# A fused attention and MLP kernel: another split of the last token tile, another wait ahead of the weight loads, and another ranking of all planned steps

## The chip, the cores and the metric

One core of a Trainium2 chip runs the kernel. The metric is device time in microseconds (us), the median of eight runs. The profile is one more execution, taken by the hardware profiler. Engines are named as the profile names them: PE is TensorE with its matmuls, PEld its weight loads, DVE is VectorE, ACT is ScalarE, POOL is GpSimd, SP is SyncE (which here only issues DMAs). L1124 is line 1124 of the kernel before.

## The reference, cut to what matters

Block-sparse causal attention over 4 batches of 8 heads, 768 tokens and 64 columns a head, and then an MLP over the 3072 tokens.

```python
k_rep = k.reshape(B, H, 12, 64, D).mean(axis=3)          # mean of each block of 64 keys
gate = einsum('bhsd,bhnd->bhsn', q, k_rep), causal by block, else -1e9
# each query attends to its own block and to the 3 best blocks by gate, causally
attn = softmax(where(mask, q @ k.T / 8, -1e9)) @ v
x = attn as [3072, 512]
out = gelu_tanh(x @ w_in) @ w_out                        # 512 -> 2048 -> 512
```

## The kernel before, in words

**Stages.** Heads are worked in pairs; p = 0 to 3 are the pairs of batch 0, 4 to 7 those of batch 1, and so on. For each batch there are three stages.

- *Preparation of a pair* (`pre`): k and q come in as float32 by DMA (`load`, tiles `ksd`, `qsd`, `vsd`), are transposed on DVE (L585) or, in batch 0, mostly on PE (L566, L569). DVE sums k by block (L628), PE makes the gate scores (L693), DVE picks the best blocks (L709 to L730, the `sel` chain), and the mask is turned by PE (L762) or by a DMA transpose (L769). POOL, DVE and ACT cast k, q and v to 16 bits.
- *Attention of a pair* (`heads2` in batch 0: PE L866, ACT L885, PE L934; `heads` afterwards: PE L1049 scores, ACT L1062 exponentials, POOL L1076 diagonal masking, PE L1088 times v, DVE L971/L972 division). The result is transposed into `xT` (L991 on PE, or L996 by DMA).
- *MLP of a batch*: `s1` is x times w_in with Gelu (PE L1124, 128 matmuls a batch; ACT L1136). The second product is `s2_plain` in batch 0 (PE L1206, 96 matmuls) and `s2` in batches 1 to 3. `s2` works with seven half-size products a pair of token tiles instead of eight; DVE makes the sums of operands they need (L1176 for w_out, L1194 for the activations), PE the products (L1254, seven "halves" of 8 matmuls of 256 columns for each token pair), and DVE joins them (L395 for one copy, L1298 for the joins) into the output tile `osb`, which SP stores (L1331).

Scores and first MLP products go into two double-width PSUM tiles (`wide`), everything else of PE into four single PSUM banks (`bank`).

**What sets the order.** Each step is added to a planner (`Plan`) with its engines, an estimated cost, the steps that it depends on, and the buffers that it takes and gives. The planner walks the steps in simulated time, always taking, of those that can start first, the one with the lowest rank; the ranks are a list of constants, `RANK`, one for each step. What comes out is one order for each engine's queue, written out in advance. On the chip each queue runs strictly in that order: an instruction that waits holds up all that is behind it on its engine.

**Fillers.** `warm` (L1351) adds 72 matmuls of 256 columns that multiply an identity and whose result nobody reads. They have the last rank of all, so the planner puts one wherever it believes PE to have nothing else to do, until the 72 are used up. On the chip they are instructions like others and take their place in PE's queue.

**Loads and their gates.** SP issues nearly all loads. The two weight loads go through POOL's DMA queue (`load_w`, L485), w_in in two halves of DFF and w_out in two halves of its rows. The first half of each is preceded by a small POOL copy that reads a landed tile (L482), v of pair 3 for w_in and q of pair 4 for w_out, so that the weight load is issued only once that tile has landed. SP in turn holds the next loads behind a small DMA that reads the first half of the weights (`hold`, L493). For pair 4, q is issued ahead of k: SP has q of pair 4 from 35.88 us and k from 40.16 us, and POOL issues w_out at 40.71 us.

**The last token pair.** In `s2` the seven halves of a token pair run on PE in the order 1, 5, 2, 6, 3, 4, 7 over two banks, P and Q. The joins are: `a_e` copies product 1 to `osb`; `eo` adds product 5; `bo` (after half 6) adds to both quarters of the first row block; `co` (after half 4) and `do` (after half 7) finish the four quarters. Half 3 waits for `eo`, since it overwrites a half bank that `eo` reads. `co` ends the first token tile and `do` the second; each tile is stored whole (256 KB) by SP.

Of the kernel before, what the change touches and what calls it, by code (L numbers as in the profile page):

```python
# [21 lines left out]
    165, 130, 222, 240, 129, 241, 103, 211, 111, 84, 211, 61, 51, 212, 293,  # L22
    65, 212, 231, 42, 284, 32, 3, 284, 39, 4, 283, 49, 650, 1, 285, 121, 29,
    285, 71, 30, 284, 48, 394, 18, 286, 90, 26, 286, 110, 139, 285, 158,
    368, 138, 286, 60, 355, 28, 642, 624, 324, 73, 519, 522, 326, 105, 352,
    72, 99, 67, 1018, 377, 83, 496, 380, 82, 107, 24, 36, 76, 164, 162, 56,
    373, 91, 85, 81, 13, 89, 168, 86, 34, 190, 1029, 449, 971, 156, 102,
    100, 52, 381, 346, 75, 429, 416, 117, 118, 621, 313, 114, 113, 827, 298,
    514, 261, 178, 186, 384, 273, 188, 479, 361, 309, 134, 534, 271, 209,
    199, 396, 424, 198, 392, 189, 136, 115, 575, 214, 109, 140, 453, 142,  # L30
    756, 141, 494, 120, 639, 174, 232, 295, 233, 15, 163, 557, 35, 58, 557,
    43, 351, 300, 428, 300, 19, 171, 135, 148, 239, 315, 254, 101, 108, 526,
    378, 362, 314, 206, 490, 182, 552, 379, 180, 296, 451, 312, 512, 345,
    289, 548, 311, 169, 393, 318, 194, 74, 170, 365, 316, 339, 181, 172,
    383, 317, 395, 237, 63, 504, 319, 275, 382, 260, 729, 247, 290, 421,
    288, 643, 272, 353, 277, 281, 55, 448, 246, 320, 347, 524, 610, 208,
    195, 244, 503, 616, 521, 226, 310, 336, 1098, 390, 341, 364, 333, 573,
    155, 269, 299, 358, 323, 482, 527, 553, 321, 488, 425, 253, 200, 335,
    350, 363, 297, 294, 680, 1271, 1270, 388, 54, 98, 322, 668, 264, 343,
    78, 325, 203, 95, 359, 354, 786, 357, 789, 520, 434, 509, 342, 467, 437,  # L40
    790, 389, 93, 782, 435, 44, 334, 258, 469, 80, 565, 344, 399, 77, 413,
    837, 414, 94, 41, 557, 251, 259, 149, 774, 776, 775, 797, 582, 64, 1439,
    1003, 550, 933, 934, 794, 11, 38, 125, 502, 505, 619, 1019, 529, 66,
    263, 577, 431, 433, 709, 221, 474, 498, 407, 412, 470, 397, 452, 436,
    473, 307, 947, 608, 723, 1233, 147, 1332, 1342, 945, 1313, 625, 948,
    843, 841, 928, 144, 736, 759, 611, 765, 478, 764, 713, 766, 936, 438,
    688, 955, 670, 737, 724, 653, 967, 1034, 1442, 252, 654, 1090, 607, 833,
    193, 951, 862, 950, 1310, 532, 823, 769, 1275, 1013, 97, 493, 1111, 536,
    444, 992, 531, 644, 618, 578, 215, 712, 663, 767, 783, 822, 1016, 798,
    1267, 924, 1491, 1512, 1408, 1407, 689, 844, 1216, 8, 213, 1200, 958,  # L50
    838, 940, 1091, 944, 969, 792, 793, 282, 265, 242, 305, 587, 651, 655,
    507, 419, 561, 703, 705, 728, 640, 959, 960, 785, 1070, 1184, 1182,
    1249, 201, 204, 205, 248, 262, 104, 249, 677, 686, 697, 719, 707, 661,
    750, 385, 386, 622, 540, 544, 546, 492, 614, 491, 338, 374, 268, 303,
    515, 517, 617, 612, 631, 635, 641, 460, 443, 463, 462, 458, 456, 555,
    687, 1017, 835, 1187, 267, 500, 143, 202, 183, 176, 349, 450, 486, 487,
    735, 747, 748, 1163, 1160, 1541, 572, 483, 1208, 440, 441, 484, 331,
    411, 806, 814, 706, 191, 497, 511, 855, 585, 468, 648, 851, 746, 623,
    613, 1062, 14, 235, 600, 682, 1064, 784, 132, 153, 1183, 849, 131, 700,
    666, 229, 696, 306, 791, 404, 472, 558, 45, 695, 558, 23, 606, 558, 53,  # L60
    694, 228, 37, 57, 40, 423, 238, 420, 699, 308, 541, 398, 400, 1066, 12,
    79, 250, 157, 197, 123, 658, 681, 207, 154, 725, 704, 702, 243, 768,
    543, 302, 664, 173, 757, 698, 701, 236, 669, 376, 678, 96, 636, 568,
    372, 406, 518, 586, 538, 192, 559, 27, 391, 559, 33, 216, 559, 47, 758,
    22, 21, 882, 150, 223, 220, 224, 665, 369, 913, 909, 230, 660, 124, 270,
    62, 175, 601, 119, 234, 405, 567, 50, 445, 551, 615, 432, 861, 638, 69,
    489, 889, 799, 426, 632, 566, 159, 459, 634, 562, 278, 554, 570, 1068,
    605, 749, 480, 917, 304, 560, 46, 161, 560, 31, 255, 560, 25, 225, 196,
    122, 771, 772, 166, 184, 167, 513, 218, 337, 872, 874, 633, 70, 564,
    177, 301, 455, 563, 466, 684, 457, 1079, 576, 753, 446, 811, 464, 942,  # L70
    584, 754, 877, 1734, 348, 581, 807, 910, 447, 943, 1311, 179, 360, 371,
    692, 547, 744, 340, 593, 592, 387, 595, 1540, 780, 185, 755, 859, 580,
    495, 481, 740, 287, 367, 210, 579, 596, 628, 589, 501, 442, 1222, 1225,
    1304, 824, 817, 809, 921, 1026, 925, 603, 927, 962, 1377, 961, 996, 781,
    1086, 1320, 923, 868, 860, 926, 691, 1354, 330, 329, 773, 1110, 1143,
    994, 998, 1317, 717, 734, 821, 836, 1380, 1083, 1085, 1103, 1134, 1256,
    597, 796, 667, 718, 1274, 328, 332, 733, 815, 953, 898, 869, 974, 1294,
    1132, 883, 919, 1159, 1539, 1228, 1231, 1567, 952, 1072, 1157, 939,
    1234, 1232, 499, 409, 410, 731, 832, 972, 1717, 1105, 1106, 1578, 1643,
    1664, 1683, 732, 770, 1658, 1728, 1727, 1648, 1645, 1253, 1735, 1492,  # L80
    803, 1287, 1358, 1494, 1631, 1646, 1603, 1661, 1653, 858, 1640, 1715,
    1718, 1714, 886, 187, 356, 16, 1639, 847, 1171, 716, 714, 863, 675, 676,
    829, 867, 1028, 1048, 1080, 893, 894, 891, 887, 941, 761, 1047, 1137,
    1056, 1206, 1331, 1333, 1336, 1052, 762, 1381, 1379, 1378, 1454, 1099,
    1337, 620, 5, 1375, 935, 984, 1081, 1084, 1089, 1189, 1082, 1154, 1053,
    1168, 599, 1076, 476, 475, 528, 604, 477, 1051, 1421, 1322, 1343, 1374,
    970, 1403, 1361, 1447, 1071, 1515, 1520, 1365, 1584, 1104, 116, 227, 20,
    133, 890, 1738, 127, 890, 1742, 92, 890, 1749, 465, 375, 68, 146, 145,
    1009, 1069, 523, 598, 1015, 1199, 506, 1197, 657, 739, 1224, 471, 266,
    1308, 1542, 1186, 1156, 918, 1535, 1528, 916, 1245, 1627, 1666, 826,  # L90
    1142, 1329, 760, 1152, 1012, 1366, 1607, 1153, 530, 1041, 1543, 1282,
    549, 973, 1513, 831, 1219, 880, 978, 1357, 1000, 106, 892, 1741, 257,
    892, 1736, 126, 892, 1737, 788, 590, 370, 777, 778, 1097, 854, 545, 583,
    556, 1223, 1094, 1095, 418, 741, 804, 805, 864, 1496, 1511, 1155, 1014,
    1630, 1536, 1061, 1005, 1716, 1626, 1131, 1007, 1656, 991, 1531, 1642,
    1006, 673, 1522, 1063, 1024, 674, 1655, 1411, 1151, 846, 875, 292, 920,
    1165, 1135, 1301, 510, 895, 1748, 662, 895, 1733, 571, 895, 1750, 1725,
    1207, 439, 1675, 1676, 1205, 659, 485, 937, 1312, 1353, 1214, 1591, 276,
    742, 876, 871, 693, 1266, 881, 828, 1409, 884, 1025, 911, 914, 1055,
    1045, 839, 904, 1376, 1010, 1044, 813, 902, 1373, 853, 800, 1410, 908,  # L100
    845, 1399, 915, 1074, 1011, 626, 965, 1243, 820, 1020, 245, 896, 1744,
    88, 896, 1739, 763, 896, 1686, 1446, 1246, 1299, 1315, 1316, 1300, 1075,
    1302, 1732, 852, 857, 327, 1254, 217, 743, 993, 1021, 679, 1633, 1042,
    1367, 810, 1278, 1073, 1178, 866, 1321, 1067, 1326, 801, 1166, 1118,
    1078, 1037, 1453, 525, 1077, 1038, 1196, 602, 1280, 1150, 1050, 981,
    1284, 968, 1400, 1594, 1319, 537, 726, 1437, 1436, 1033, 1261, 656, 897,
    819, 976, 1001, 899, 906, 929, 999, 903, 722, 721, 720, 975, 963, 1696,
    1684, 1705, 1721, 1123, 1124, 1065, 1140, 1369, 1167, 1209, 1176, 1175,
    1713, 1251, 997, 995, 1255, 1711, 1148, 1088, 985, 1161, 1710, 1194,
    1114, 1726, 1036, 1141, 1059, 1096, 1147, 1722, 1144, 1113, 1146, 1172,  # L110
    1709, 1174, 1139, 1138, 1252, 1712, 1297, 1277, 1305, 1328, 1707, 1035,
    1745, 988, 990, 1002, 1115, 949, 1125, 1370, 1330, 1335, 1334, 1339,
# [69 lines left out]
class Plan:  # L182
# [12 lines left out]
    def add(self, *a, **kw):  # L195
        op = Op(*a, **kw)
        self.ops.append(op)
        return op
# [81 lines left out]
def kernel(  # L280
# [9 lines left out]
    nc = tc.nc  # L290
# [950 lines left out]
    def s2(b):  # L1241
# [95 lines left out]
        for t in range(NC // 2):  # L1337
            token(t)
# [107 lines left out]
```

## Time and profile before

| | |
|---|---|
| median of 8 runs | 259.37 us (258.5 to 262.62) |
| profiled execution, its own time | 258.56 us |
| its span in the profile | 256.7 us |
| PE busy | 251.4 us, 98% |
| DVE, ACT, POOL busy | 179.4, 162.8, 86.2 us |
| loads and stores | 32.63 MB, mean 127 GB/s |
| L1124, L1254, L1206, L1049 matmuls | 512, 504, 96, 192 |
| L1351 fillers | 72 |

The profiled execution's time is 1.86 us more than its span: what lies around the program. A matmul's duration in the profile covers its passage through the array and overlaps the next one, so the distance of starts is what it costs PE: 18 fillers in a row took 2.13 us, of which the last one 0.27, hence 0.109 us each. For the same reason a short wait of PE does not always show as idle time.

### The profile page before, as it was taken

Reading aid. Unit: us, or ns where it says so; the run is one execution under the profiler, and the core shown is the slowest. Engines: PE = TensorE matmul, PEld = TensorE weight load, DVE = VectorE, ACT = ScalarE, POOL = GpSimd, SP = SyncE. Lnnn points to the kernel's source line nnn. Section 1 sums busy time; section 2 is a strip of 40 time slices with the busy share of each in tenths; the row PEclk is TensorE's granted clock in tenths of the full one; section 3 lists DMA queues with packets and bytes.
Section 4 is the critical chain, followed back from the end, with each engine's and each line's share of the span. In section 5 each row is a group of like instructions: output and inputs, shape, how many; then the busy total and the mean of one; then the engine's idle time right before and its main releaser. Section 6 shows DMA issues by size and latency. Waiting matters only on the chain.

```text
span 256.7 us, 6482 instructions
## 1 busy us (share of the span) xinstructions
PE 251.4 (98%) x2530; PEld 175.1 (68%) x2530; DVE 179.4 (70%) x525; ACT 162.8 (63%) x204; POOL 86.2 (34%) x168
## 2 busy tenths in 40 slices
PE   6999999999999999999999999999999999999996
PEld 5877676555456665555778786556878896567885
DVE  1897865031899999999999999997844452308542
ACT  2278777656678995567798396556898843664000
POOL 8755824011556575404153753010144310000000
PEclk9999999999999999999999999999999999999999
DMA  8998998999898889999895792312021142000222
GB/s 163 218 147 179 175 215 120 201 215 192 166 192 176 179 138 177 199 196 188 137 186 110 136 230 61 107 28 51 1 84 33 41 105 83 3 0 0 84 82 84
DMA packets 133951, 32.63 MB, mean 127 GB/s; under 512 B 127680, under 2 KB 129824, under 8 KB 133920
## 3 DMA queue, kind: packets, MB, share of 16 engines
q1 hardware_dynamic: 129184, 27.62, 54.2%
q0 software_dynamic: 3136, 4.19, 9.8%
q10 hardware_dynamic: 1600, 0.39, 0.8%
q8 instruction: 20, 0.33, 0.6%
q14 instruction: 11, 0.09, 0.1%
HBM read 27.26 MB, written 6.29 MB: 131 GB/s over the span
## 4 chain that ended last, share of the span: by engine, by line
PE 82%; DVE 12%; POOL 3%; issue 1%; ACT 1%; DVEq 0%; POOLq 0%
PE wide L1124 33%; PE bank L1254 18%; PE wide L1049 8%; PE bank L1206 6%; PE bank L1088 4%; PE wide L866 3%; PE bank L934 2%; PE bank L693 2%; DVE qT L395 2%; PE bank L1351 2%; DVE sel L725 1%; PE bank L566 1%; DVE osb L1298 1%; PE bank L991 1%; PE bank L762 1%
## 5 line engine op out<-in xcount | busy, mean ns | idle before, releaser
L1124 PE MATMUL wide<-xT,w_in 128*128 128x384 f16 x512 | 87.3, 326 | 0.0
L1136 ACT ACTIVATE G<-wide 128x768 f16<-128x768 f32 x64 | 51.8, 811 | 42.3 <-PE wide L1124 41.7
L1124 PEld LDWEIGHTS <-w_in 128*128 128x128 f16 x512 | 49.5, 98 | 33.0 <-issue 1.3
L1062 ACT ACTIVATE at<-wide 128x896 f16<-128x896 f32 x72 | 62.4, 916 | 12.5 <-PE wide L1049 10.4
L1076 POOL TENSOR_SCALAR_AFFINE_SELECT at<-at 128x256 f16<-128x256 f16 x72 | 31.4, 437 | 60.1 <-ACT at L1062 59.2
L1049 PE MATMUL wide<-qT,kT 76*128 76x512 f16 (+3 forms) x192 | 38.2, 305 | 0.3 <-DVE qT L395 0.3
L393 POOL CAST kT<-k 64x768 f16<-64x768 f32 x20 | 17.3, 868 | 43.4 <-DVE k L585 42.4
L1254 PEld LDWEIGHTS <-G 128*128 128x128 f16 x288 | 27.1, 97 | 5.2 <-issue 0.5
L1254 PE MATMUL bank<-w_out,G 128*128 128x256 f16 x216 | 30.1, 272 | 0.3 <-DVE osb L1298 0.3
L1298 DVE TENSOR_TENSOR osb<-bank,osb 128x512 f32<-128x512 f32 (+1 forms) x36 | 22.1, 617 | 11.1 <-PE bank L1254 10.6
L1206 PE MATMUL bank<-w_out,G 128*128 128x512 f16 x96 | 27.0, 379 | 0.0
L1088 PEld LDWEIGHTS <-at 128*128 128x128 f16 x504 | 21.8, 98 | 4.1
L1049 PEld LDWEIGHTS <-kT 76*128 76x128 f16 x192 | 17.1, 98 | 10.5 <-issue 1.1
L885 ACT ACTIVATE at<-wide 128x1024 f16<-128x1024 f32 (+3 forms) x24 | 20.8, 917 | 4.8 <-PE wide L866 4.7
L1088 PE MATMUL bank<-v,at 128*128 128x65 f16 x504 | 23.8, 194 | 0.0
L1254 PEld LDWEIGHTS <-XS 128*128 128x128 f16 x216 | 20.3, 98 | 3.1 <-DVE zr L971 0.3
L1254 PE MATMUL bank<-TS,XS 128*128 128x256 f16 x144 | 20.8, 272 | 0.0
L585 DVE STREAM_TRANSPOSE k<-ksd 128x768 f32<-128x768 f32 x12 | 11.5, 967 | 10.6 <-DMA ksd<-in_k_dram 10.6
L1194 DVE TENSOR_TENSOR XS<-G 128x768 f16<-128x768 f16 x12 | 7.2, 603 | 16.1 <-ACT G L1136 16.0
L1351 PE MATMUL bank<-ident 128*128 128x256 f16 x72 | 12.9, 302 | 2.3 <-DVE ident L323 2.3
L972 DVE TENSOR_TENSOR xn<-bank,zr 128x384 f16<-128x384 f32 x24 | 13.4, 557 | 0.8
L725 DVE MAX8 sel<-sel 128x8 f32<-128x12 f32 x160 | 13.2, 157 | 0.6
(97 smaller groups left out, 316.4 us busy)
## 6 DMA issues: line engine op xcount, KB each, us to landing
out_dram<-osb SPq DMA_DIRECT2D x24, 256.0 KB, 2.7
vsd<-in_v_dram SPq DMA_DIRECT2D x26, 192.0 KB, 3.2
qsd<-in_q_dram SPq DMA_DIRECT2D x48, 96.0 KB, 2.6
ksd<-in_k_dram SPq DMA_DIRECT2D x48, 96.0 KB, 3.0
w_in<-in_moe_w_in_dram POOLq DMA_DIRECT2D x2, 1024.0 KB, 11.6
w_out<-in_moe_w_out_dram POOLq DMA_DIRECT2D x2, 1024.0 KB, 12.8
G<-in_k_dram SPq DMA_DIRECT2D x4, 192.0 KB
G<-in_v_dram SPq DMA_DIRECT2D x4, 192.0 KB, 4.5
```

The costliest lines, as they stand in the source:

```text
L393: nc.gpsimd.tensor_copy(out=out, in_=in_)
L885: nc.scalar.activation(out=T["at", u][:, :, 0:n], in_=plan.buf[("st",) + u].rearrange("p (h w) -> p h w", h=2)[:, :, 0:n], func=AF.Exp, bi ...
L1049: nc.tensor.matmul(st[:, x:e], kT16[i][h][0:76, s0:s0 + 128], qT16[i][h][0:76, s0 + (x - cb):s0 + (e - cb)], start=True, stop=True)
L1062: nc.scalar.activation(out=T["at", u][:, 0:n], in_=plan.buf[("st",) + u][:, 0:n], func=AF.Exp, bias=0.0, scale=SCALE)
L1076: nc.gpsimd.affine_select(out=dg, in_=dg, compare_op=ALU.is_ge, fill=0.0, base=0, pattern=[[0, 2], [1, 128]], channel_multiplier=-1)
L1088: nc.tensor.matmul(pvv[:, qc, 0:65], at[:, cb + (qc - jc) * 128: cb + (qc - jc + 1) * 128], v16[i][:, jc, h, :], start=(gi == 0 and jc == ...
L1124: nc.tensor.matmul(hps[:, 512 * e:512 * e + HALF], w_in16[:, ci, (2 * j + e) * 128: (2 * j + e + 1) * 128], T["xT", b][:, ci, HALF * h:HAL ...
L1136: nc.scalar.activation(out=G[:, :, h, j, :], in_=plan.buf["hps", b, j, h].rearrange("p (e w) -> p e w", e=2)[:, :, 0:HALF], func=AF.Gelu_a ...
L1206: nc.tensor.matmul(plan.buf["ops", b, ti], G[:, f % 2, 2 * ti // NC, f // 2, ti % (NC // 2) * 128:ti % (NC // 2) * 128 + 128], w_out16[:, ...
L1254: nc.tensor.matmul(dst[:, HD * h:HD * h + HD], FACT[m][0][:, j, t * 128:(t + 1) * 128], FACT[m][1][:, j, :], start=(clear and j == 0), sto ...
L1298: nc.vector.tensor_tensor(out=dst(), in0=src(), in1=other(), op=ALU.add)
L1351: nc.tensor.matmul(plan.buf["warm", n][:, 0:256], ident16, z, start=True, stop=True)
```

## The change

Three things are changed.

**The order.** All of `RANK` is replaced (1776 numbers before, 1779 after, since the last token pair has other steps). The queues that come out differ almost from the start. What the later text speaks of, in the queues of the changed kernel:

- SP issues k of pair 1 ahead of q of pair 1, v of pair 2 ahead of v of pair 3, and k of pair 4 ahead of q of pair 4.
- On POOL the copy that gates w_in follows the cast of v of pair 2; the copy that gates w_out follows the cast of k of pair 4, for one head.
- On PE the `s1` matmuls of batch 0 come nearly as one block (118 of 128 before the first L1206), all 96 L1206 matmuls come before the first `s1` matmul of batch 1, and the fillers lie elsewhere: 47 before the first `s1` matmul of batch 0 (48 in the kernel before), 3 in that stage, 22 around the end of batch 1's attention and the first 16 `s1` matmuls of batch 1, and none after that. The kernel before has 2 fillers after batch 1's `s1`, 4 in the last `s2`, and 18 behind its last real matmul.
- ACT does 12 of the casts of q (8 before), DVE 12 (16 before).

**The load gates.** `T["latest"]` is the tile of the load emitted last, and the gating copy reads that, in two pieces of 8 elements at opposite ends of it. In the planner w_in now depends on v of all four pairs, not of pair 3 alone. In the order that comes out, the tiles read are those of before: v of pair 3 and q of pair 4.

**The last token pair.** The halves of the last one run in the order 1, 5, 6, 3, 4, 7, 2, with half 2 alone in a third bank, R. Product 1 is copied to another quarter and half 2 is joined last, as one quarter (256 columns). The stores: the second quarter of the first tile (128 KB) by SP, the whole second tile (256 KB) by ACT's queue, then the first quarter of the first tile (128 KB) by SP.

```diff
-            T[key, p] = sd
+            T[key, p] = T["latest"] = sd
...
                 x = const.tile([1, 16], FP32, name=f"after_{name}")
-                nc.gpsimd.tensor_copy(out=x, in_=T[after][0:1, 0, 0, 0:16]
-                                      if len(T[after].shape) == 4 else
-                                      T[after][0:1, 0, 0:16])
+                y = T["latest"]
+                for n, z in ((0, y[0:1, 0]), (8, y[96:97, y.shape[1] - 1])):
+                    if len(y.shape) == 4:
+                        z = z[:, n // 8]
+                    nc.gpsimd.tensor_copy(out=x[:, n:n + 8], in_=z[:, 0:8])
             nc.gpsimd.dma_start(out=dst[part], in_=view[part])
...
+            if b == B - 1 and t == NC // 2 - 1:
+                return ending(half, quad, two, bank_of, a_e, join, key, post)
...
+        def ending(half, quad, two, bank_of, a_e, join, key, post):
...
+            half(1, "P", 1, True, [])
+            mm = half(5, "P", 0, False, [])
...
+            ao = add({DVE: 0.45, ACT: 0.45}, a0_e, [mm], post,
+                     takes=("osb", ("osb", key)))
+            eo = add({DVE: 0.34}, join(
+                lambda: quad(3), of("P", 0), lambda: quad(0)), [ao], post)
+            mm = half(6, "Q", 1, True, [])
+            bo = add({DVE: 0.34}, join(
+                lambda: quad(1), of("Q", 1), lambda: quad(0)), [mm, ao], post)
+            half(3, "P", 0, False, [eo])
+            mm = half(4, "P", 1, True, [])
+            go = add({DVE: 0.34}, join(
+                lambda: quad(2), of("P", 1), lambda: quad(0)), [mm], post)
+            co = add({DVE: 0.34}, join(
+                lambda: quad(1), of("P", 0), lambda: quad(1)), [mm, bo], post,
+                gives=[])
...
+            store([co], 0, 1, 2, SP)
+            mm = half(7, "Q", 1, False, [bo])
+            do = add({DVE: 0.66}, join(
+                lambda: quad(2, 2),
+                lambda: two(bank_of("Q")[:, HD:2 * HD]).to_broadcast(
+                    [128, 2, HD]),
+                lambda: quad(2, 2)), [mm, go, eo], post)
+            store([do], 1, 0, 2, ACT)
+            mm = half(2, "R", 0, True, [])
+            last_op = add({DVE: 0.34}, join(
+                lambda: quad(0), of("R", 0), lambda: quad(0)), [mm, do], post)
+            store([last_op], 0, 0, 1, SP)
...
-            [ld["v", 3]], -200 + x, None if x else ("v", 3))
+            [ld["v", x] for x in range(HP)], -200 + x, None if x else "v")
```

## The prediction

> **What bounds the kernel now.** I read the busy shares first, then the stages (busy time by windows), then the fillers alone, then the waits, then the timeline of the end.
>
> ```profile
> PE 251.4 (98%) x2530; PEld 175.1 (68%) x2530; DVE 179.4 (70%) x525; ACT 162.8 (63%) x204; POOL 86.2 (34%) x168
> PE   6999999999999999999999999999999999999996
> DVE  1897865031899999999999999997844452308542
> PEclk9999999999999999999999999999999999999999
> ```
>
> PE is busy from 2.3 us to the last product at full clock, so the time is what stands in PE's queue, plus its waits, plus head and tail. DVE is the second bound from about 60 to 147 us.
>
> The fillers (L1351, PE only) by windows; columns are the window, its length, busy time and count, clock, DMA share and GB/s:
>
> ```profile
> 0.00:5.20 5.20, 2.92 (x14) 1.00 0.74 150
> 5.20:38.60 33.40, 6.82 (x36) 1.00 1.06 188
> 38.60:123.20 84.60, 0.03 (x1) 1.00 1.00 179
> 123.20:234.80 111.60, 0.38 (x2) 1.00 0.36 79
> 234.80:252.47 17.67, 0.60 (x4) 1.00 0.16 61
> 252.47:256.70 4.23, 2.13 (x18) 1.00 0.32 124
> ```
>
> A filler that straddles a border counts in both windows. By the queue, 48 lie before batch 0's first L1124, 6 later, and 18 behind the last real product, where they cost nothing.
>
> PE's waits in the middle are short. In the timeline (start, duration, row) two show:
>
> ```profile
> 74.48 0.59 PE L1206 MATMUL bank<-w_out,G 128*128 128x512 f16 x2
> 75.36 0.54 PE L1049 MATMUL wide<-qT,kT 76*128 76x512 f16 x3 [0.29 <-DVE qT L395]
> 143.89 1.03 PE L1254 MATMUL bank<-TS,G 128*128 128x256 f16 x8
> 145.26 0.60 PE L1254 MATMUL bank<-w_out,G 128*128 128x256 f16 x4 [0.33 <-DVE osb L1298]
> ```
>
> By starts (0.216 us for an L1206, 0.109 for an L1254) PE lost 0.45 us before 75.36 and 0.50 before 145.26. Three more gaps found the same way, near 66.7, 68.9 and 78.9, make 0.5. So the middle loses 1.45 us besides 6 fillers (0.65). Both named waits are on DVE.
>
> **The fillers: +1.96 us.** No real matmul is added or removed; only the order differs. All 72 fillers now lie before the last real product instead of 54. PE runs its queue in order, so 18 x 0.109 = 1.96 us is spent ahead of the end, whatever else happens. The question is what waits these fillers, and the new order, take away.
>
> **Head: 0.** 47 fillers instead of 48 before the first `s1` product. The first 14 wait for the same k transfer (first L566 at 5.24). k of pair 1 comes first, so attention can start earlier than 13.52, but ACT paces what follows (20.3 us busy of the 25.1 from 13.5 to 38.6). Early gaps of PE sum to about 0.7; between losing and doubling them lies -0.7 to +0.7. I take 0, since the filler count is nearly the same.
>
> **Gate of w_in: 0.** The tile read is the same. SP issues v of pair 2 first, two DMAs (1.09 us), and POOL has one more cast (0.83) ahead; a second small copy adds up to 0.19. So w_in goes out 1.1 to 2 us after 25.39. Its first half had landed by 35.26 and is first needed at 38.6: 3.3 us cover. If that cover were gone, PE would pay the excess, at most 2 us.
>
> **Gate of w_out and k of pair 4 first.** Before:
>
> ```profile
> DVE k L585 <- DMA ksd<-in_k_dram: 10.6, 1, 10.6
> 40.16 2.27 SPq L427 DMA_DIRECT2D ksd<-in_k_dram  x4
> 51.35 0.56 SPq L493 DMA_DIRECT2D held_out<-w_out  x1
> 53.17 4.84 SPq L427 DMA_DIRECT2D ksd<-in_k_dram  x4
> ```
>
> k of pair 4 shared the DMA engines with w_out and DVE got it at 55.24. Now both loads land first: k where q did, near 40.6, so DVE transposes it about 42.5 and pair 4 is prepared some 12 us earlier. But POOL's w_out issue stands behind q's landing (q issue ends at 42.4, +0.5 as before: about 43) and behind the k cast (42.5 + 0.97 DVE + 0.82 POOL = 44.3). So w_out goes at about 44.5, not 40.71: +3.8. Having the engines to itself it gives back about 1, so SP's gate opens near 54 instead of 51.35 and pair 5's loads start 3 us later. First use of w_out moves later too: behind 118 L1124, 38.6 + 118 x 0.163 + 2 for what is between = 60 against a landing near 55, so PE doesn't wait for it.
>
> On DVE, pair 5's k transpose is queued behind the copy of the first plain token tile, which needs 128 L1124 and 16 L1206: 38.6 + 20.9 + 3.5 + 3 for other products = 66.0, then 0.69. Pair 5 starts on DVE at 66.6; before it was 64.92. From there DVE paces batch 1 (32.6 us busy of 35.4 between 62.3 and 97.7): last exponential at 97.68 before, at 99 to 100.5 now. PE meanwhile has spent all its L1206; before, 9 were left (12 counted from 97.7, some started) to cover the chain from the last exponential through masking (0.4), v product, division (0.75), turn, copy (0.8) and first Gelu at 102.33. The 22 fillers stand exactly there, 2.4 us. I estimate the hole at 2.5 to 4: the uncovered part is 0.1 to 1.6; I take 0.7. The sum counts the fillers once.
>
> **DVE afterwards.** Four q casts go to ACT (DVE -2.2 us, ACT +3.3 at 0.55 and 0.83), which ACT's 10 us idle between 97.7 and 123.2 can hide. DVE is behind by 1 to 2 us at the start of batch 2 but has more of its w_out sums done. The old 1.45 us of waits may go; waits of the same kind may come. From 0 to 2.5 us; I take 0.5, near the old 145 us row.
>
> By the Trainium skill (TensorE: Matmul & The Clock Gate, HAM oscillation) PE idle over about 3 us drops its clock, which speaks against having no filler after the first 16 products of batch 1. The row says otherwise: the longest middle wait is 0.5 and the clock row stays at 9. By the row this costs 0; by the rule a hole of that size costs about 1.7 more (3.4 us at half clock). I take 0 and keep 1.7 for the upper end.
>
> **Last `s2` start: +0.4.** Four fillers used to fill the wait for the last Gelu and DVE sums; that chain is unchanged, so about 0.44 of wait comes back in their place.
>
> **The ending: -0.2.**
>
> ```profile
> 247.24 1.04 PE L1254 MATMUL bank<-TS,XS 128*128 128x256 f16 x8
> 248.11 1.04 PE L1254 MATMUL bank<-w_out,G 128*128 128x256 f16 x8
> 248.31 0.42 DVE L395 COPY osb<-bank 128x256 f32<-128x256 f32 x1 [1.05 <-PE bank L1254]
> 248.77 0.42 DVE L1298 TENSOR_TENSOR osb<-bank,osb 128x256 f32<-128x256 f32 x1
> 252.68 0.69 DVE L1298 TENSOR_TENSOR osb<-bank,osb 128x512 f32<-128x512 f32 x1 [0.18 <-PE bank L1254]
> ```
>
> Half 5 starts at 247.24; copy and join end at 249.19, and half 3 must wait for that. Two halves (2 x 0.87) covered it; now only half 6 does, so half 3, due at 248.98, waits 0.27 with the semaphore. The last join is 0.42 instead of 0.69: 0.27 back. What remains is the store. It is issued at 253.40, and in the answer by windows the DMA engines move its 256 KB from 254.24 to 255.30. By the row, half the bytes save 0.5. By the skill (DMA: Bandwidth & Descriptors, Issuing engines are not separate DMA queues) ACT's store, issued about 0.6 earlier, runs on the same engines and interleaves, so the last two stores together have nearly the old bytes left: 0.1. I take 0.2.
>
> **Sum.** +1.96 - 1.45 + 0.7 + 0.5 + 0.4 - 0.2 = +1.9, on the profiled execution 258.56 + 1.9 = 260.5. The median of the runs is 0.81 above the profiled one; on it, 259.37 + 1.9 = 261.3.
>
> **Rivals.** A measurement tells a change from none at about 0.5%, 1.3 us.
>
> - *Main: a hole at the end of batch 1's attention that fillers only dress up.* 261.3; 260.7 to 263. For it: all L1206 are used up before. 0.56.
> - *The early k pays (the other side, not slower).* Pair 4 is ready 12 us earlier, DVE keeps that lead, and PE waits nowhere beyond its fillers: +1.96 - 1.45 + 0.4 - 0.2 = +0.7, or 260.1; with early gaps gone too, 259.4. It decides if the last exponential of batch 1 ends by about 98. For it: DVE idled 10.6 us for this k. Against: pair 5 is later. 0.32. Its best case, with a full 0.5 of store and no wait at all, is 258.7; over 0.5% faster is left only to scatter.
> - *Late w_out.* If w_out, issued at 44.5, takes its old two-load time under pair 4's last packets and lands after 60, PE stalls at the first L1206 and SP's later loads slide with it: +3 more, 264.3. Against: the engines are free then. 0.10.
> - *The change doesn't do what it says*: the gates read the same tiles as before, so nothing but the order and the ending acts: 259.4. 0.02, and part of the second.
>
> Range 258.9 to 264.0: the low end is near the second's best case, the high end takes in uncovered hole and batch 2 waits (+0.9, +2.0) and reaches the third. Faster 0.05, same 0.33, slower 0.62.
>
> **What would show it.** k of pair 4 on DVE near 42.5; w_out issued near 44.5; pair 5's k near 66.6; last exponential of batch 1 near 100, fillers in a block there with PE idle beside them; half 3 of the last pair waiting 0.27; last join 0.42. Wrong if the first Gelu of batch 1 comes before 102.3, or if PE shows waits over 1 us elsewhere, above all at the first L1206 or in batch 2.

## The result, and the profile after

The changed kernel takes 262.04 us (median, 261.29 to 263.2) where the kernel before takes 259.45 beside it: ratio 1.0105, 95% interval 1.008 to 1.0131. It is slower by 2.6 us of medians; 261.3 was forecast, from 258.9 to 264.0. The profiled executions lie further apart: 262.18 us with a span of 260.5, against 258.56 and 256.7, so 3.6.

The busy shares of the changed kernel and two rows of its slices:

```profile
PE 252.5 (97%) x2530; PEld 174.6 (67%) x2530; DVE 178.8 (69%) x523; ACT 166.0 (64%) x209; POOL 86.9 (33%) x169
PE   6999999999999999999999999999999999999994
PEclk9999999999999999999999999999999999999999
```

PE is still the bound and its clock stays at full. The fillers (now L1403) by windows. The columns are those of the same view of before, with one more behind PE's count, PEld's busy time and count:

```profile
5.20:40.20 35.00, 6.64 (x35) 2.57 (x33) 1.00 0.96 170
40.20:102.10 61.90, 1.38 (x7) 0.60 (x7) 1.00 0.95 173
102.10:126.50 24.40, 2.82 (x19) 1.76 (x18) 1.00 0.98 184
126.50:252.80 126.30, 0.00 (x0) 0.00 (x0) 1.00 0.35 80
```

All 72 lie before 126 us. Since PE runs its queue in order, its time can be accounted for completely: from each instruction's start to the next, less what that kind takes when nothing holds it (0.162 us for an L1126, 0.216 for an L1208, 0.109 for a filler). What is left over is lost. From PE's first transposition at 5.24 us, in us, before and after (each stage runs to the start of the next instruction; the columns add up to the length within 0.2 us):

| stage | length | products | fillers | lost |
|---|---|---|---|---|
| head, to batch 0's first `s1` product | 33.2, 35.0 | 23.2, 23.7 | 3.68, 3.57 | 6.15, 7.50 |
| `s1` of batch 0, attention of batch 1 | 59.5, 61.9 | 57.7, 59.2 | 0, 0.75 | 1.80, 1.97 |
| `s1` of batch 1 | 25.0, 25.0 | 24.6, 22.0 | 0, 1.95 | 0.36, 1.03 |
| from there to the last `s2` | 110.7, 110.9 | 108.7, 109.3 | 0.22, 0 | 1.81, 1.55 |
| last `s2`, to its last product | 18.7, 18.6 | 18.2, 18.1 | 0.43, 0 | 0.17, 0.57 |
| sum | 247.1, 251.4 | 232.4, 232.3 | 4.33, 6.27 | 10.3, 12.6 |

The last product starts 4.28 us later: 1.94 of fillers and 2.33 of lost time, more than half of that (1.35) in the head. Behind the last product 0.5 comes back. PE's longest waits in the changed kernel, without the one at the very start (what waits, for what, total, times, longest; by starts each costs 0.1 to 0.2 more):

```profile
PE bank L764 <- DVE madd L732: 0.5, 1, 0.5
PE wide L1051 <- DVE qT L395: 0.5, 1, 0.5
PE bank L1090 <- POOL at L1078: 0.4, 1, 0.4
PE bank L936 <- POOL at L913: 0.2, 1, 0.2
PE bank L993 <- DVE xn L955: 0.2, 1, 0.2
PE bank L1090 <- DVE xn L974: 0.2, 1, 0.2
```

By starts, the first costs 0.69 us at 12.73, in the head. The third costs 0.59 at 100.44, at the end of batch 1's attention, for POOL's masking. The second costs 0.66 at 126.33: behind the last `s1` product of batch 1, PE waits for DVE's copy of q before the first scores of batch 2. This one wait is the 0.67 us by which the third row of the table rose; where the fillers stand, PE loses no more than before.

The loads of pairs 4 and 5 on SP's queue. In the planner w_out now depends on k and q of pair 4, where before it depended on q alone; that is part of the change too.

```profile
37.42 0.58 SPq L495 DMA_DIRECT2D held_in<-w_in  x1
38.04 5.38 SPq L427 DMA_DIRECT2D ksd<-in_k_dram  x4
58.59 0.57 SPq L495 DMA_DIRECT2D held_out<-w_out  x1
60.42 4.64 SPq L427 DMA_DIRECT2D ksd<-in_k_dram  x4
```

k of pair 4 reaches DVE at 45.37 us, not 42.5; w_out is issued at 48.38, not 44.5; SP's gate opens at 58.6, not 54; pair 5's k is on DVE at 67.83, not 66.6. On POOL, w_in's gate stands behind a cast of q as well as the cast of v that I had counted:

```profile
26.93 0.41 POOL L913 TENSOR_SCALAR_AFFINE_SELECT at<-at 128x256 f16<-128x256 f16 x1 [2.40 <-ACT at L887]
27.29 0.82 POOL L393 CAST XS<-q 128x768 f16<-128x768 f32 x1
28.06 0.83 POOL L393 CAST v<-TS 128x768 f16<-128x768 f32 x1
28.83 0.42 POOL L486 COPY after_in<-vsd 1x8 f32<-1x8 f32 x2
29.19 0.92 POOL L487 DMA_DIRECT2D w_in<-in_moe_w_in_dram  x1
```

It goes out 3.8 us later than before, and DMA is nearly idle meanwhile (48 GB/s in that slice of the page). PE doesn't wait for it, but SP does: the hold behind w_in's first half opens at 37.42 us instead of 35.26, and k of pair 4 is issued that much later than q was before (38.04 instead of 35.88). PE never waits for w_out at its first plain product (61.18 us).

Where the lead of pair 4 went is seen on ACT, first in the changed kernel, then in the one before (start, duration, row; L1064 and L1062 are the exponentials):

```profile
69.88 1.73 ACT L1064 ACTIVATE at<-wide 128x896 f16<-128x896 f32 x2 [0.27 <-PE wide L1051]
73.28 0.59 ACT L391 COPY osb<-bank 128x512 f32<-128x512 f32 x1 [1.67 <-PE bank L1208]
...
80.83 3.60 ACT L1064 ACTIVATE at<-wide 128x896 f16<-128x896 f32 x4 [1.21 <-PE wide L1051]
...
96.34 4.99 ACT L1064 ACTIVATE at<-wide 128x896 f16<-128x896 f32 x6 [0.99 <-PE wide L1051]
```

```profile
70.51 3.57 ACT L1062 ACTIVATE at<-wide 128x896 f16<-128x896 f32 x4 [0.62 <-PE wide L1049]
74.11 0.68 ACT L391 COPY qT<-bank 12x640 f16<-12x640 f16 x1
76.00 1.73 ACT L1062 ACTIVATE at<-wide 128x896 f16<-128x896 f32 x2 [1.21 <-PE wide L1049]
...
95.95 1.73 ACT L1062 ACTIVATE at<-wide 128x896 f16<-128x896 f32 x2
```

Pair 4 was ready early, but in the queues its first scores come at 63.23 us (PE), and its exponentials stand behind ACT's last Gelu of batch 0, which ends at 64.24. Then, from 71.6 to 80.8 us, ACT has no exponential at all, where before the gap is 74.1 to 76.0. The last six follow each other without a pause and end at 101.33 us (before 97.67). By then PE has no plain product left; the first Gelu of batch 1 comes at 106.26 (before 102.33).

The end, with half 3 (the PEld row) and the joins:

```profile
252.34 0.42 DVE L395 COPY osb<-bank 128x256 f32<-128x256 f32 x1 [1.05 <-PE bank L1256]
252.79 0.84 DVE L1300 TENSOR_TENSOR osb<-bank,osb 128x256 f32<-128x256 f32 x2
253.27 0.75 PEld L1256 LDWEIGHTS <-XS 128*128 128x128 f16 x7 [0.27 <-issue]
256.81 0.37 ACTq L1344 DMA_DIRECT2D out_dram<-osb  x1
256.96 0.42 DVE L1300 TENSOR_TENSOR osb<-bank,osb 128x256 f32<-128x256 f32 x1 [0.18 <-PE bank L1256]
```

Half 3 waits 0.27 us and the last join takes 0.42, both as forecast. What lies behind the last product's start falls from 4.33 to 3.85 us.

### The profile page after: what moved, and what is told of

Its sections match the earlier page's. It is cut to its first block, busy times and chain, and to the rows that moved or that the text cites. A ratio compares the mean times of both kernels' runs of the same rounds, so it can differ in the third digit from the quotient of the medians.

```text
span 260.5 us, 6480 instructions
## 1 busy us (share of the span) xinstructions
PE 252.5 (97%) x2530; PEld 174.6 (67%) x2530; DVE 178.8 (69%) x523; ACT 166.0 (64%) x209; POOL 86.9 (33%) x169
## 4 chain that ended last, share of the span: by engine, by line
PE 75%; DVE 15%; DMA 4%; POOL 2%; issue 2%; ACT 1%; SPq 1%; DVEq 0%; POOLq 0%; ACTq 0%
PE wide L1126 24%; PE bank L1256 18%; PE wide L1051 8%; PE bank L1208 7%; PE bank L1090 4%; PE wide L868 3%; PE bank L1403 3%; PE bank L695 2%; DMA vsd<-in_v_dram 2%; DVE q L587 2%; DVE XS L1196 2%; PE bank L936 2%; DVE qT L395 2%; DVE osb L1300 1%; DVE XS L395 1%
## 5 line engine op out<-in xcount | busy, mean ns | idle before, releaser
L1126 PE MATMUL wide<-xT,w_in 128*128 128x384 f16 x512 | 87.0, 326 | 0.0
L1064 ACT ACTIVATE at<-wide 128x896 f16<-128x896 f32 x72 | 62.0, 916 | 14.2 <-PE wide L1051 10.4
L1126 PEld LDWEIGHTS <-w_in 128*128 128x128 f16 x512 | 49.2, 98 | 32.2 <-issue 1.3
L1078 POOL TENSOR_SCALAR_AFFINE_SELECT at<-at 128x256 f16<-128x256 f16 x72 | 32.2, 449 | 79.1 <-ACT at L1064 78.7
L1300 DVE TENSOR_TENSOR osb<-bank,osb 128x512 f32<-128x512 f32 (+1 forms) x38 | 22.4, 591 | 12.6 <-PE bank L1256 11.9
L1208 PE MATMUL bank<-w_out,G 128*128 128x512 f16 x96 | 26.3, 379 | 0.0
L393 POOL CAST kT<-k 64x768 f16<-64x768 f32 x19 | 16.0, 843 | 27.5 <-DVE k L587 26.1
L1403 PE MATMUL bank<-ident 128*128 128x256 f16 x72 | 13.8, 302 | 2.3 <-DVE ident L323 2.3
L393 POOL CAST v<-vsd 128x768 f16<-128x768 f32 x13 | 12.8, 984 | 5.0 <-DMA vsd<-in_v_dram 4.7
```

The costliest lines, as they stand in the source:

```text
L393: nc.gpsimd.tensor_copy(out=out, in_=in_)
L1064: nc.scalar.activation(out=T["at", u][:, 0:n], in_=plan.buf[("st",) + u][:, 0:n], func=AF.Exp, bias=0.0, scale=SCALE)
L1078: nc.gpsimd.affine_select(out=dg, in_=dg, compare_op=ALU.is_ge, fill=0.0, base=0, pattern=[[0, 2], [1, 128]], channel_multiplier=-1)
L1126: nc.tensor.matmul(hps[:, 512 * e:512 * e + HALF], w_in16[:, ci, (2 * j + e) * 128: (2 * j + e + 1) * 128], T["xT", b][:, ci, HALF * h:HAL ...
L1208: nc.tensor.matmul(plan.buf["ops", b, ti], G[:, f % 2, 2 * ti // NC, f // 2, ti % (NC // 2) * 128:ti % (NC // 2) * 128 + 128], w_out16[:, ...
L1300: nc.vector.tensor_tensor(out=dst(), in0=src(), in1=other(), op=ALU.add)
```

## The experiments

Medians are quoted with the ratio to the kernel before and its interval. Medians of different calls are compared by their ratios. In the mixtures of orders the planner is given a fixed list of steps and engines instead of ranks; their diff is then the one line, and the list is told in words:

```diff
-    order = plan.solve()
+    order = plan.solve([(int(x[1:]), NAMES[x[0]]) for x in FORCED.split()])
```

### The ending, without and alone

`e1_no_ending` is the changed kernel with the old steps of the last token pair, `e2_ending_alone` the kernel before with the new ones.

```diff
-            if b == B - 1 and t == NC // 2 - 1:
-                return ending(half, quad, two, bank_of, a_e, join, key, post)
```

> The changed order with the old ending of the last token tile (halves 3 and 4 in the old places, one store of the whole row block). By the two traces the new ending costs half 3 a wait of 0.26 us and gives 0.5 us back behind the last product, so without it the kernel should take 0.25 us more than the changed kernel: 262.3, ratio 1.011, last join 0.69, no wait at half 3. A rival holds that the last tile is where the loss is (half 3's wait, two stores from two queues): then this kernel falls back to 259.4 to 260. Everything ahead of 250 us should be as in the changed kernel: first Gelu of batch 1 at 106.3.

> The old order and the old gates with only the new ending of the last token tile. If the ending is worth a net -0.25 us (half 3 waits 0.26, the part behind the last product is 0.5 shorter), this takes 259.2, ratio 0.999; the tail behind the last product should go from 4.08 to about 3.56. If the ending is what costs, it takes 260.5 or more. Last exponential of batch 1 as in the kernel before, at 97.7.

Without the ending: 262.37 us, 1.0113 (1.0086 to 1.014). The ending alone: 259.33, 0.9995 (0.997 to 1.002). The difference of 0.0008 to the changed kernel and that of 0.0005 to the kernel before have the forecast sign and lie inside the intervals. The ending isn't the loss.

### The fillers of the hole

```diff
-                nc.tensor.matmul(plan.buf["warm", n][:, 0:256], ident16, z,
-                                 start=True, stop=True)
+                if n < 50:
+                    nc.tensor.matmul(plan.buf["warm", n][:, 0:256], ident16,
+                                     z, start=True, stop=True)
```

> The changed kernel with the last 22 of its 72 fillers (those between the 16th plain product of batch 1 and the end, around 99 to 107 us) left out; they write scratch banks only and are not part of what is computed. Theory A (the last exponential of batch 1 comes late and fillers merely stand in the hole): time unchanged within 0.5 us, 261.6 to 262.1, PE shows about 2.4 us more of waits between 99 and 107 us, the first Gelu of batch 1 again near 106, and the clock row stays at 9. Theory B (each filler in the queue costs its 0.109 us): 259.6 to 259.9, first Gelu near 104.

261.76 us, 1.009 (1.0059 to 1.0121): theory A's time. In the trace, first `s1` product to last product takes 215.62 us instead of 216.44, so 0.82 of 2.40. The other 1.6 turned into waits: in `s1` of batch 1 PE now loses 2.43 us, where with the fillers it lost 1.03 beside 1.95 of fillers. By starts, four new waits between 102.9 and 107.9 us make 1.96 (0.40, 0.40, 0.74, 0.42), while the wait before batch 2's first scores shrinks from 0.66 to 0.23. So at least two thirds of the fillers stood in a real hole of about 2 us. The waits that appear:

```profile
PE wide L1126 <- ACT G L1138: 0.6, 1, 0.6
PE bank L695 <- DVE ksb L647: 0.3, 1, 0.3
PE wide L1126 <- ACT xT L391: 0.2, 1, 0.2
PE bank L993 <- DVE xn L974: 0.2, 1, 0.2
```

The clock stays at 1.00 between 95 and 107 us, so the rule of the Trainium skill that I weighed (TensorE: Matmul & The Clock Gate, HAM oscillation: a drop after some 3 us without work) had nothing to bite on: no single wait there is longer than 0.74.

### Earlier gates

```diff
+    for op in gate["in"] + gate["out"]:
+        order.remove(op)
+    at = order.index(spot["q16", 3][0])
+    order[at:at] = gate["in"]
+    at = order.index(issued["q", HP]) + 1
+    order[at:at] = gate["out"]
```

> The changed kernel with both gates of the weight loads moved ahead on POOL: the two gate copies and the loads of w_in stand before the q cast of pair 3 and the v cast of pair 2 instead of behind them, those of w_out before the k casts of pair 4. Theory A (the late start of the chain of pairs 5 to 7 is the loss, and the gates set it): w_in is issued near 25.5 instead of 29.2, k of pair 4 is on DVE near 42 instead of 45.4, w_out goes out near 45 instead of 48.4, the last exponential of batch 1 ends 1 to 3 us earlier (98.5 to 100.3) and the time falls by 0.5 to 2.5 us, to 259.5 to 261.5. Theory B (the fillers and the head are the whole loss): no change, 261.8 to 262.3. Between the two: DVE's copy of the first plain token tile stands ahead of pair 5's k and waits for PE until about 67 us; if that alone holds pair 5, the gates are early and the last exponential stays at 101.

261.80 us, 1.0094 (1.0066 to 1.0121): no change that can be told. But the edit did less than it was meant to: w_in went out at 28.31, not 25.5, because its copy now waited for POOL's masking in front of it and then for v; w_out went at 47.93 instead of 48.38, k of pair 4 was on DVE at 44.53 instead of 45.37. Pair 5's k stayed at 67.90, behind the copy of the first plain tile. That gates don't matter isn't shown by this run; that pair 5 doesn't follow them is.

### Which part of the order: the head or the rest

`e5_old_head_new_rest` takes the kernel before's order up to its first `s1` step and the changed order from there; `e6_new_head_old_rest` the reverse. Both have the old ending.

> Old ending and, up to batch 0's first s1 product, the order of the kernel before on every engine (with its early w_in load); from there on the changed kernel's order, k of pair 4 ahead of q included. In the trace of the changed kernel PE reached batch 0's first s1 product 1.74 us later, 1.35 of it in waits. If the head is a lasting part of the loss, this kernel starts s1 near 38.5 and keeps that to the end: 261.0 (1.4 below the kernel with the changed order and the old ending, 262.37), ratio 1.0055. If the head's loss is swallowed by the later hole (the last exponential of batch 1 comes late for another reason), it stays at 262 or more and fillers and waits near 100 us take the difference.

> The reverse: the changed kernel's order up to batch 0's first s1 product, then the order of the kernel before (q of pair 4 ahead of k, old places of the fillers, old ending). If the head costs its 1.35 us of waits and nothing later gives them back: 260.9, ratio 1.0052, first s1 product near 40.2. If the later order is the whole loss: 259.6.

The new head alone: 260.47 us, 1.0042 (1.0026 to 1.0057). It starts `s1` at 40.07 and keeps all of that to the end: from there to the last product takes 213.87 us, in the kernel before 213.90. So the head costs about 1.05 us of medians, and by subtraction the rest of the change the other 1.5; no run gives the rest alone. In this run w_in goes out late too (28.72 us), and SP's hold opens at 37.13; the old order behind it takes no longer for that.

The old head with the new rest: 262.24, 1.0113 (1.0081 to 1.0145), as if the head were worth nothing. Its trace says that it wasn't the old head: `s1` starts at 39.85, since the seam put 0.49 us of products and a wait of 0.27 in front, and one DVE instruction took 0.84 us instead of 0.20 (told at the end). From there the time is the changed kernel's: 216.18 us, which is what e1, with the same ending, takes (216.16).

### Pair 5 early, with and without the late fillers

PE's queue is the changed kernel's, row for row. SP's loads of v of pair 4 and k and q of pair 5 no longer wait for w_out, and DVE turns them ahead of the first plain copy.

```diff
+        on = held[p > HP + 1]
         if p > HP:
-            load(p, "k", held[1])
-            load(p, "q", held[1])
-        load(p, "v", held[1])
+            load(p, "k", on)
+            load(p, "q", on)
+        load(p, "v", on)
```

> The changed kernel with PE's, ACT's and POOL's queues untouched; SP issues the loads of v of pair 4 and k and q of pair 5 without waiting for w_out, and DVE transposes and sums pair 5's k and q ahead of the copy of the first plain token tile. Theory A (DVE's late start on pair 5, at 67.8 us, makes the hole at the end of batch 1's attention): pair 5's k is on DVE near 60, PE's waits between 63 and 107 us (2.5 us in all in the changed kernel) shrink to about 1, and the time falls by 1 to 1.5 us to 260.5 to 261, the 22 fillers still in the queue. Theory C (PE's own queue sets the last exponential, DVE only follows): waits and time stay, 261.8 to 262.3. The loads share the engines with w_out; should w_out land after 61.2 us, PE waits at the first plain product and that wait is to be taken off.

> The kernel of the run before it with the last 22 fillers left out (they write scratch banks only). In the changed kernel leaving them out gave 1.2 us in the profiled span, half of their 2.4, since the other half stood in the hole. Theory A: with pair 5 early the hole is gone, so the fillers cost what they take: 2.0 to 2.4 below the run before it, about 258.5. Theory C: about 1.2 below it, 260.5 to 261.

262.55 us, 1.0114 (1.0082 to 1.0146): by the waits and the time, theory C, though 0.25 above its figures. Without the late fillers 262.29, 1.0113 (1.008 to 1.0147): a miss for both theories, since C too had asked for 260.5 to 261. In its trace the part from the first `s1` product to the last product is 1.26 us shorter than with them (215.55, 216.81), but `s1` starts 0.46 later, and the medians differ by 0.26 alone. In the first of the two, DVE has pair 5's k 6.1 us and its q 3.6 us earlier, and what follows comes no earlier (the last row at 76.22 us, in the changed kernel at 75.73):

```profile
61.71 0.98 DVE L572 STREAM_TRANSPOSE k<-ksd 128x768 f32<-128x768 f32 x1 [3.97 <-DMA ksd<-in_k_dram]
66.88 0.98 DVE L572 STREAM_TRANSPOSE q<-qsd 128x768 f32<-128x768 f32 x1 [2.64 <-DMA qsd<-in_q_dram]
73.12 0.20 DVE L958 RECIPROCAL zr<-bank 128x6 f32<-128x6 f32 x1 [4.54 <-PE bank L1075]
76.22 0.35 DVE L696 STREAM_TRANSPOSE sel<-bank 128x160 f32<-128x160 f32 x1 [1.02 <-PE bank L680]
```

DVE idles 4.5 us for PE's products with v of pair 4, and then for pair 5's gate product (here L680), which PE's queue has at 75 us, in the changed kernel behind 23 plain products that come after 67.6. In the kernel before, that product is picked up by DVE at 70.77. It is thus the place of a few products in PE's queue that starts pair 5, not DVE and not the loads; what an earlier place for them would gain was not run. My step "pair 5's k transpose is queued behind the copy" was true and didn't matter.

### Plain products into the hole

The last eight plain products (L1208) of batch 0 are moved from 94 to 99 us into the places of the late fillers, their copy and store behind them. The expectation has these 22 fillers left out; in the kernel that ran they are still there, behind the last real product.

> The changed kernel with the last 22 fillers left out (scratch only) and, in their places between 101 and 107 us of PE's queue, the last eight products of the last plain token tile of batch 0 (8 x 0.216 = 1.73 us), which the changed order spends at 94 to 99 us, ahead of the last scores; that tile's copy, store and the second half of the w_out sums follow them. Theory C (PE's own queue sets the last exponential, and the hole is there because all plain products are spent before it): the last exponential of batch 1 ends about 1.7 us earlier than with the fillers left out alone (99.3 instead of 100.9), PE's waits in s1 of batch 1 fall from 2.4 us to about 1, and the time is 1.2 to 1.7 below that kernel's 261.76: 260.0 to 260.6. Rival (DVE's chain of pairs 6 and 7 sets it): PE waits for DVE ahead of the last scores instead, the last exponential stays near 101 and the time at 261.5 to 262.

> The same, and with the kernel before's order on every engine up to 44 us, past batch 0's first s1 products (pair 4's two loads and the w_out load keep the changed order), so that the seam of the first such mixture, 0.49 us of products moved ahead and a wait of 0.27, is gone. If the head is worth its 1.35 us of waits: first s1 product near 38.5 and 1.1 to 1.5 below the run before this one, 258.6 to 259.4, level with the kernel before or up to 0.3% under it. If the head's gain is swallowed later: 260 or more.

265.06 us, 1.0212 (1.0173 to 1.0251): both theories fail, and the trace names three reasons (L1036 are the scores, L1049 the exponentials, L680 a gate product):

```profile
97.15 0.54 PE L1036 MATMUL wide<-qT,kT 76*128 76x512 f16 x3 [0.25 <-ACT at L1049]
97.96 0.54 PE L1036 MATMUL wide<-qT,kT 76*128 76x512 f16 x3 [0.27 <-ACT at L1049]
98.77 0.54 PE L1036 MATMUL wide<-qT,kT 76*128 76x512 f16 x3 [0.27 <-ACT at L1049]
109.92 0.34 PE L680 MATMUL bank<-q,ksb 128*32 128x160 f32 x4 [1.75 <-DVE ksb L632]
```

With eight products fewer ahead of them, the last scores wait for ACT, once for each exponential; the last of these ends at 101.15 us, 61.3 behind the first `s1` product, where it was 61.1 in the changed kernel. So over its last 5 us this stage follows ACT, at 0.82 us an exponential, and the plain products there had been cover. The second reason is of my making: on DVE the moved copy waits 1.46 us for its products, batch 2's block sums are queued behind it, and PE pays 1.75 us. The third lies at the end: SP waits 2.8 us for the last stores to land where it waited 1.4, and what lies behind the last product's start grows from 3.8 to 5.25 us. Whether the fillers there cause it is not shown: they end 1.0 us before the stores have landed, and 15 of them in the same place in `e2` lengthened nothing. So what the move of the eight products alone costs is not shown.

`e10` was to have the old head too. Its kernel is e9's, line for line, so its expectation was not put to the test: 265.59, 1.0212 (1.0164 to 1.026).

### The ending without the fillers of the middle

The kernel before with the new ending and with fillers 48 to 71 left out, by the condition shown above with 48.

> The kernel before with the new ending and with fillers 48 to 71 left out: six stood between batch 0's s1 and the end (0.65 us), 18 behind the last product. If the six cost their time: 258.7, ratio 0.997, the clock row still at 9. If they stood in waits: 259.3, as with the ending alone.

258.48 us, 0.9958 (0.9923 to 0.9994), the only version that is faster than both kernels, if barely than the one before. With the new ending nine fillers, not six, stand ahead of the last product (0.98 us). From first `s1` product to last product takes 213.65 us instead of 214.20 in e2: 0.55 of 0.98 is gained, the rest turns into waits.

### The old head once more

The kernel before's order on every engine up to about 42 us, past the first `s1` products, then the changed order and its ending.

> The kernel before's order and w_in gate on every engine up to about 42 us, past batch 0's first s1 products; from there on the changed kernel's order, with k of pair 4 ahead of q, all its fillers and its ending. It mends the seam of the first such mixture, which had moved 0.49 us of products ahead and added waits, and so started s1 at 39.85. If the head's loss is real and lasting, the first s1 product comes at 38.4 to 39.0, the rest takes the changed kernel's 216.4 us from there to the last product, and the time is 1.0 to 1.5 below the changed kernel: 260.5 to 261.1, ratio 1.004 to 1.007. If later waits swallow it, 261.8 or more.

263.23 us, 1.0156 (1.0119 to 1.0192): a miss, and inconclusive. `s1` starts at 39.65, and two new waits of 0.9 (44.5 us) and 0.8 us (56.4), for the Gelu and for the mask of pair 4, belong to the seam. An order cannot be cut at the head without a new one behind it. What the changed order would take with the old head stays open; what the new head costs in front of the old order is e6.

## Why the prediction came out as it did

- **Fillers, +1.96.** The count was right (+1.94 in the queue). "Whatever else happens" was not: leaving 22 out gives back 0.82 of 2.40 in the trace, and by the ratios (1.0105, 1.009) about 0.4 us, which the intervals don't separate from nothing.
- **Head, 0.** The step that failed: "I take 0, since the filler count is nearly the same." Fillers fell by 0.11, lost time rose by 1.35, and e6 gives 1.05 of medians. Attention did start earlier (first scores at 11.03 us, not 13.52), but its last scores end the head later, at 39.16 instead of 37.9. PE's three longest waits there from 10 us on are 0.69 us for a mask and 0.36 and 0.34 between 24 and 28 us, where the old head has 0.29, 0.24 and 0.23; the rest is spread over shorter ones. (Most of the 6.15 us lost before are distances of about 0.1 us between products of different kinds.) I bounded the head by its waits before, when what mattered was a new order of them. Which of the moved steps makes these waits stays open.
- **Gate of w_in, 0.** Its time was wrong (3.8 us later, not 1.1 to 2), since I counted the cast of v and not the cast of q in front of it. PE doesn't wait for it in the profiled execution. That SP waits behind it, I had left out.
- **Early k.** The four times of the loads came 1.2 to 4.6 us after those I named, 2.2 of it from w_in's late gate. The rival "the early k pays" falls: the last exponential ends at 101.33, not by 98. The rival "late w_out" falls too: its first product doesn't wait.
- **Hole, +0.7 beyond fillers.** The place and the kind were right: plain products all spent, and in e3 a hole of about 2 us where the fillers had stood. The fillers cover it whole; what is uncovered is the 0.59 us for POOL's masking at 100.44, between them. The cause I gave, DVE pacing pair 5, was wrong (e7): PE's order starts pair 5 late, and ACT paces the last six exponentials.
- **Old waits, -1.45, and new ones.** The old ones are gone. From the first `s1` product up to the last `s2`, those that came in their places make 2.06 us (0.18, 0.16, 0.15, 0.59, 0.66, 0.32), where the sum had 1.2, the hole's 0.7 and 0.5 for DVE.
- **DVE afterwards, +0.5; last `s2`, +0.4.** Batch 2 waits for DVE at 126.33 (0.66) and at 156.02 (0.32), where it had waited 0.50 at 144.65: the term was of the right kind and too small. The wait at the last `s2`'s start is 0.13.
- **Ending, -0.2.** -0.5 behind the last product and +0.26 at half 3. The last join gives 0.27 of the 0.5, which leaves 0.2 to the stores: what I took between the row's 0.5 and the 0.1 of the skill's rule on issuing engines (DMA: Bandwidth & Descriptors, Issuing engines are not separate DMA queues), and nearer to the rule.

By the terms, the profiled execution was forecast at +1.9 and came at +3.6: about 1.3 of the difference is the head, 0.9 the new waits behind it, and the last `s2` takes 0.3 off again. The medians came at +2.6, so the forecast looks better on them than its terms are: the profiled execution of the kernel before lies 0.9 us under its median, that of the changed kernel 0.1 above. The range held because its upper end had 2.7 us of room for waits without cover, and waits of another place used 0.7 of it. That is in part luck.

## What to carry to other kernels

A wait can't be subtracted because its cause is moved: a new order brings waits of its own, and where a stage's order is new its cost can't be taken from the old stage's gaps. A filler in an in-order queue costs its time only where the engine would have had work; count the products that could cover a hole before pricing it. And before an early input is called a gain, follow it to the first instruction that needs it in each queue: here it was a handful of gate products placed late on PE.

## What the runs showed of the hardware

**A few hundredths of a microsecond decide 0.6 us.** In the old head a DVE instruction of two inputs and a POOL cast start within 0.1 us of each other. In e2 and then in e5:

```profile
11.04 0.20 DVE L711 TENSOR_TENSOR sel<-sel,cgate 128x48 f32<-128x48 f32 x1
11.05 0.87 POOL L388 CAST XS<-q 128x768 f16<-128x768 f32 x1
```

```profile
11.05 0.82 POOL L378 CAST XS<-q 128x768 f16<-128x768 f32 x1
11.10 0.84 DVE L701 TENSOR_TENSOR sel<-sel,cgate 128x48 f32<-128x48 f32 x1
```

Where DVE starts 0.05 us or more after POOL (e5) it takes 0.84 us, about as long as the cast; e11 and e12 show the same, 0.10 us after. In e2 and in the kernel before, where it starts within 0.02, it takes 0.20. It recurs later, as in the kernel before, POOL's row first:

```profile
30.52 0.83 POOL L393 CAST v<-TS 128x768 f16<-128x768 f32 x1
30.77 0.70 DVE L726 TENSOR_TENSOR sel<-sel,sel 128x120 f32<-128x120 f32 x1
```

Without a cast beside it the same instruction takes 0.28 us (at 64.40); here it ends 0.1 us behind the cast. One that reads a PSUM bank and starts with a cast (`xn<-bank,zr`, 26.32 us) keeps its 0.56. The Trainium skill (GPSIMD Engine Reference, Specifications) says that the two engines contend for SBUF when a DVE instruction has two inputs there. That this is the cause wasn't tried; it fits. With it the old head ends at 38.44 us (e2) or 39.04 (e11), which may be part of why the two profiled executions lie 3.6 us apart and the medians 2.6.

**A clock that falls without a long wait.** In e10, the same kernel as e9, the granted clock (third figure from the right) halves for some 3 us, after four waits of 0.41 to 0.43 us by starts; in e9, with the same waits, it stays at 1.00:

```profile
97.00:99.00 2.00, 1.23 (x11) 0.63 (x8) 1.97 (x5) 2.00 (x4) 1.52 (x3) 1.00 0.61 97
99.00:101.00 2.00, 1.65 (x16) 0.91 (x16) 2.00 (x3) 2.00 (x3) 2.00 (x4) 0.84 1.00 161
101.00:103.00 2.00, 2.00 (x31) 1.65 (x30) 1.97 (x5) 1.88 (x3) 0.57 (x2) 0.50 0.77 158
103.00:105.00 2.00, 2.00 (x17) 1.10 (x15) 1.11 (x4) 0.00 (x0) 0.00 (x0) 0.80 1.18 229
```

So the clock can fall where no wait in the 4 us before is longer than 0.43 us, in one execution and not in another of the same kernel. That the short waits are the reason is suggested by their place alone.
